# Four LayerNorm tiles on ScalarE, one softmax sum on VectorE, and a new instruction order in a fused attention and token-mixing block

## The chip, the core and the metric

The kernel runs on one core of one Trainium2 chip. The metric is device time in microseconds (us) of one execution. Six executions of the kernel before the change took 207.69 to 209.28 us, with a median of 208.07 us.

## The reference

All inputs are bfloat16. There is one batch, S = 2048 positions and D = 512 features.

```python
mod = (silu(c) @ w_mod).reshape(1, 6, 1, 512)        # sa, ca, ga, sb, cb, gb
h = layernorm(x) * (1 + ca) + sa
x = x + ga * A(h)                                     # A: sliding attention
h = layernorm(x) * (1 + cb) + sb
x = x + gb * B(h)                                     # B: MLP over positions

def A(x):   # 32 heads of 16; each position looks at 8 positions: itself and 2, 4 .. 14 before it
    q, k, v = split(x @ wqkv)
    logits = einsum('bhsd,bhswd->bhsw', q, kg) * 16 ** -0.5    # positions before 0 masked
    return einsum('bhsw,bhswd->bhsd', softmax(logits), vg) @ wo

def B(x):
    h = layernorm(x)
    u = gelu(einsum('bsd,sf->bdf', h, w1) + b1)       # F = 1792, the sum runs over positions
    return (einsum('bdf,fs->bds', u, w2) + b2).transpose(0, 2, 1)
```

So there are three norms in a row: the first feeds the attention, the second follows it, and the third is the one inside B. Because B sums over all positions, its first product can begin for early positions while the attention of later positions is still being computed.

## The kernel before

The 2048 positions are 16 tiles of 128. They are worked in five chunks of 2, 4, 4, 4 and 2 tiles (`SIZES`). A chunk of four tiles has 512 columns, one of two tiles has 256. Each step is added to a graph under a name with its engine (`G.add`, lines 50 to 83); in the names the first number is a tile, a chunk, or a chunk and a part. For each chunk:

- `ln1s<tile>` (line 628, by `ln_stats`, line 368) takes mean and variance of a tile of x with `bn_stats` and `bn_aggr` on VectorE. `rstd1_*` (ScalarE) and `nb1_*` (VectorE) make scale and bias of a group, and `n1_<tile>` applies them. Which engine applies the norm of which tile is a letter in `NE` (A is ScalarE, D is VectorE, P is GpSimd).
- The tiles are transposed: in chunks 0 and 1 by TensorE (`tr*`) and copies out of PSUM (`hT*`), in chunks 2 to 4 by a transposing DMA (`xt<tile>`, line 637).
- `qkv<chunk>_<t><j>` are the products for q (t = 0), k (1) and v (2), 16 matmuls of 512 columns for four values of j in chunks 1 to 3; `ev*` copies each out of PSUM, mostly on ScalarE. `wsc<t>_<k>` scales a weight block by 1 + ca before its first use.
- `qk<chunk>_<0..3>` on VectorE multiplies q by the eight shifted copies of k, one multiply of 4096 elements a partition in a chunk of four tiles; `red*` on TensorE sums the products over the head's features. `max*` (VectorE), `sub*` (TensorE) and `exp*` (ScalarE) follow. `esum*` is the sum of the eight exponentials, made by eight matmuls with the identity, lines 766 to 769; `rcp*` (ScalarE) its reciprocal as exp(-ln), and `smB*` (VectorE) the scaling.
- `a2_*` and `vd*` are DMAs that lay out the weights and v, `pv<chunk>_<0..3>` on VectorE multiplies them, `pvacc*` on TensorE sums over the window, `oev*` (ScalarE) copies out, and `wo<tile>` is the output product plus x. `x1_<tile>` takes it out of PSUM with its row sum, `ln2q<tile>` its sum of squares (both on ScalarE, by `accum_out`), then second norm (`n2_*`, `aff*`) and third norm (`ln3s*`, `h3_*`).

B's first product is `mlp1_<part>_<ft>_<first tile>` (line 921): for 14 blocks ft of F it sums over the tiles of `h3`, in parts with parked sums (`park*`, `inj*`, `padd*`), so that it fills TensorE during the attention. `gelu<ft>` follows, then `mlp2_<tile>` over the 14 blocks, `fin<tile>` on VectorE and the store.

The order in which all engines are fed is not derived at build time: it is the text `ORDER` (line 182). `schedule` (lines 85 to 116) reads it name by name, and each engine executes its own instructions in that order. A suffix chooses the engine (`:a`, `:d`, `:p`) or, with `:q`, the form of a matmul step: `mm` (lines 500 to 504) then emits each matmul as four matmuls of 32 weight columns, on the four column strips of the array:

```python
        for j in range(0, P, 32):
            nc.tensor.matmul(out[j:j + 32], lhsT=lhsT[:, j:j + 32], rhs=rhs, tile_position=(0, j), **kw)
```

This document calls that form column-tiled, and the other plain. `red*` and `pvacc*` are column-tiled always (line 738 and line 803). The token `fill:2:114` emits 114 matmuls of 128 columns whose result nobody reads; `warm*` emits nine of these. The durations, latencies and byte counts that stand in the `add` calls are not read by `schedule`: they leave the emitted program as it is.

PSUM has six slots for matmul results (pool `ps`), and `big` has four buffers for the products of `qk*` and `pv*`; the slot of each step also follows from `ORDER`.

Of the kernel before, what the change touches and what calls it, by code (L numbers as in the profile page):

```python
# [7 lines left out]
ACT = mybir.ActivationFunctionType  # L8
# [33 lines left out]
class _Graph:  # L42
# [7 lines left out]
    def add(self, eng, dur, fn, **kw):  # L50
        return self.add_any([(eng, dur, fn)], **kw)
# [131 lines left out]
ld_x_1_2 ident ld_c act_table ld_x_1_4 ld_x0 consts warm2 ld_x_2_8 ld_x1 cps ld_x_2_6 silu_exp ld_wmod1 ln1s3  # L183
ld_wqkv1 ln1s5 ld_wqkv0 ld_x_3_10 ln1s4 ln1s2 ln1s0 rstd1_1 ln1s1 ld_wmod0 ln1s9 rstd1_0 nb1_0 nb1_1 silu_dve
n1_1 n1_0 ld_x_4_14 ln1s6 n1_5 n1_2 fill:2:114 tr0_0 ln1s8 modcols1 n1_3 halo0 ld_wqkv2 n1_4 hT0_3:a hT0_1:d
hT0_0:a ld_x_3_12 fill:4:11 tr1_2 a1col hT0_2:d wsc1_0:a wsc1_1:d tr1_0 ld_wo3 wsc1_3:d wsc1_2:d hT1_3:a ln1s7
qkv0_12 hT1_1:a ld_wmod5 wsc0_0:a wsc0_1:d qkv0_10 wsc0_3:d ld_b2 rstd1_2 wsc0_2:d ln1s10 ld_wmod4 hT1_0:a
qkv0_00 ev0_10:a ln1s11 ev0_12:a modcols0 ld_wo0 nb1_2 qkv0_02 sab hT1_2:d ld_wmod3 n1_6 qvb0 ln1s15 qkv1_02
qvb_cp0 ln1s14 wsc2_2 ev0_02:a qvb1 ln1s13 wsc2_3 qkv1_10 wsc2_1:a wsc2_0:a qvb_cp1 qk0_3 qkv1_00 ev0_00:a
qkv0_22 qk0_2 ev1_02:a qkv1_01 ev1_10:a qk0_0 qkv0_20 ev1_01:a qk0_1 ev1_00:a red0_0 xt6 qkv1_12:q n1_9 qk1_0  # L190
ev0_20:a red0_1 red0_2 ld_wo1 red0_3 mask ev1_12:a ld_wmod2 qkv1_13:q n1_7 qkv1_03 max0 n1_8 xt7 qk1_2 qkv1_11
ev1_03:a xt9 sub0 qkv1_23 ev1_11:a exp0 qkv1_21 qk1_1 ev1_13:a xt8 ev0_22:a esum0 qkv1_22:q ld_b1 rcp0 halo_v1:p
rstd1_4 vd0_1 smB0 qkv1_20 qk1_3 a2_0_1 modcol2 a2_0_0 ev1_20:a red1_0 ev1_23:a a2_0_2 red1_1 ev1_22:a red1_2
a2_0_3 ln1s12 red1_3 ev1_21:a ld_wo2 qkv2_00 mcols0 nb1_4 max1 rstd1_3 n1_14 vd0_0 n1_15 qkv2_10 vd0_2 nb1_3
ev2_00:a n1_10 sub1 pv0_1 ev2_10:a xt10 qkv2_01 n1_12 qk2_0 mrowt0 qkv2_02 exp1 vd1_3 qkv2_11 vd0_3 ev2_01:a
n1_11 vd1_2 qkv2_22 pv0_2 ev2_11:a xt12 qkv2_12 mrows0:a ev2_02:a qk2_1 pvacc0_2 xt11 ev2_12:a red2_0 n1_13
esum1:q halo_v2:p xt13 qkv2_13:q rcp1 qk2_2 ev2_22:a qkv2_03:q vd1_1 ev2_13:a qkv2_23:q ev2_03:a smB1 qkv2_20:q
qk2_3 a2_1_3 red2_1 ev2_20:a a2_1_2 qkv3_01:q halo_k3:a ev2_23:a a2_1_0 red2_2 a2_1_1 qkv3_13 pv0_0 ld_w1_0_896
red2_3 st_row0 pv0_3 ev3_13:a qkv2_21:q vd1_0 max2 pvacc0_0 ev2_21:a qkv3_10:q pv1_3 pvacc0_1 sub2:q oev0_0:a
qkv3_23:q ev3_10:a exp2 qkv3_00:q ld_row0 pv1_2 xt14 ev3_01:a qkv3_02:q ev3_00:a qkv3_20:q vd2_0 ev3_23:a vd2_1  # L200
esum2:q pv1_0 ld_w1_0_0 qkv3_21 rcp2 pvacc0_3 qkv3_03:q woq_s oev0_2:a ev3_02:a pvacc1_3 ev3_03:a smB2 qkv3_11:q
pv1_1 a2_2_2 wo1:q ev3_11:a a2_2_1 ev3_21:a wo0 xt15 x1_1 halo_v3:a qk3_1 pvacc1_1 oev1_3:a a2_2_0 pvacc1_0 x1_0
a2_2_3 qkv3_12 oev1_1:a ld_w1_0_512 oev1_0:a qk3_0 pvacc1_2 vd2_2 modcol3 oev1_2:a vd2_3 ev3_12:a ln2q0 wo4
qk3_3 wo5 x1_4 ln2q1 qkv4_12 mcols1 ev3_20:a qk3_2 red3_0 ln2q4 red3_1 qkv3_22:q ln2m0 wo3 ev3_22:a pv2_1 x1_5
mrowt1 wo2:q mrows1:a x1_3 st_row1 red3_2 pv2_0 x1_2 pvacc2_1 rstd2_0 red3_3 ln2q2 qkv4_02:q oev2_1:a ld_row1
nb2_0 max3 n2_0 vd3_3 ev4_02:a vd3_0 pv2_3 sub3 vd3_2 qkv4_10 exp3 pvacc2_0 n2_1 esum3 pv2_2 ln2q3 qkv4_20
ev4_12:a qkv4_22:q rcp3 ev4_20:a ln2m2 pvacc2_2 aff0 warm3 oev2_0:a oev2_2:a qkv4_00:q smB3 rstd2_2 ln2q5 nb2_2
pvacc2_3 ln3s0 a2_3_1 n2_2 warm1 ev4_22:a a2_3_0 ln3s1 n2_3 biascols oev2_3:a a2_3_2 ln2m4 ev4_10:a aff2 wo7:q
a2_3_3 rstd2_4 ld_w2_1 rstd3_0 wo6:q nb2_4 nb3_0 ln3s2 n2_4 n2_5 h3_0 vd3_1 ln3s3 wo8:q h3_1 x1_6 aff4 warm0
rstd3_2 x1_7 wo9:q nb3_2 ln3s4 h3_2 h3_3 x1_8 ln3s5 halo_v4:p mlp1_0_2_0:q vd4_1 ev4_00:a pv3_0 mlp1_0_5_0:q  # L210
x1_9 mlp1_0_1_0:q rstd3_4 ln2q9 mlp1_0_0_0:q nb3_4 pv3_3 biascols_cp:a vd4_2 h3_5 pvacc3_0 h3_4 mlp1_0_6_0:q
ln2q8 mlp1_0_0_4:q pv3_2 mlp1_0_1_4:q vd4_3 park0_0:a mlp1_0_5_4:q mlp1_0_2_4:q park0_1:a mlp1_0_4_0:q ln2q7
park0_2:a pv3_1 mlp1_0_3_0:q vd4_0 ln2q6 mlp1_0_3_4:q oev3_0:a pvacc3_2 park0_3:a ld_w1_0_1152 pvacc3_3 oev3_2:a
ln2m6 mlp1_0_4_4:q qk4_0 oev3_3:a pvacc3_1 rstd2_6 mlp1_0_7_0:q oev3_1:a nb2_6 qk4_2 red4_0 n2_9 mlp1_0_6_4:q
wo13:q n2_7 qk4_1 ld_w1_0_1408 n2_6 wo12:q qk4_3 n2_8 park0_4:a red4_1 red4_2 aff6 red4_3 ld_w2_3 park0_5:a
wo11:q x1_12 mlp1_0_9_0:q ln2q12 park0_6:a wo10:q max4 x1_11 ld_w2_0 ln3s8 x1_13 sub4:q mlp1_0_10_0 ln3s7 exp4
x1_10 ln3s6 esum4 mlp1_0_11_0 ln3s9 rcp4 mlp1_0_12_0 smB4 rstd3_6 ln2m12 a2_4_3 ln2q10 h3_7 mlp1_0_8_0 h3_6
a2_4_1 rstd2_12 h3_8 mlp1_0_8_4 ln2q13 a2_4_2 nb2_12 h3_9 n2_12 ln2q11 a2_4_0 ln2m13 mlp1_0_9_4 ln2m10 rstd2_13
aff12 mlp1_0_7_4 rstd2_10 nb2_10 ln2m11 mlp1_0_7_8 ln3s12 rstd2_11 mlp1_0_8_8 n2_10 mlp1_0_9_8 pv4_0
ld_w1_0_1664 mlp1_0_11_4 park0_7:a rstd3_12 nb2_13 pv4_2 mlp1_0_10_4 park0_8:a n2_13 mlp1_0_10_8 nb2_11 pv4_1  # L220
mlp1_0_11_8 park0_9:a ld_w1_1_0 mlp1_0_12_4 park0_10:a pv4_3 mlp1_0_12_8 park0_11:a pvacc4_2 pvacc4_0 park0_12:a
aff10 pvacc4_1 pvacc4_3 n2_11 mlp1_0_13_0 aff13 ld_w2_5 oev4_0:a mlp1_0_13_4 aff11 oev4_2:a mlp1_0_13_8 inj1_0
wo15 ln3s10 wo14 ln3s13 rstd3_10 ln3s11 park0_13:a mlp1_1_0_6 x1_15 ld_w1_1_640 rstd3_13 ld_w1_1_896 rstd3_11
ln2s15 inj1_4 inj1_2 inj1_3 mlp1_1_3_6 nb3_13 h3_10 rstd2_15 nb2_15 mlp1_1_2_6 x1_14 n2_15 ln2s14 h3_13
mlp1_1_3_10 inj1_1 mlp1_1_0_10 mlp1_1_1_6 aff15 rstd2_14 nb2_14 mlp1_1_2_10 ln3s15 n2_14 mlp1_1_4_6 park1_0:a
h3_12 mlp1_1_1_10 aff14 inj1_5 rstd3_15 inj1_6 mlp1_1_4_10 mlp1_1_5_6 ln3s14 ld_w1_1_1408 mlp1_1_6_6 h3_11
rstd3_14 h3_15 park1_1:a h3_14 mlp1_1_6_10 mlp1_1_5_10 park1_2:a mlp1_1_10_10 ld_w1_2_0 park1_3:a mlp1_1_9_10
park1_4:a padd1_10 park1_5:a mlp1_1_7_10 park1_6:d ld_w2_7 mlp1_1_12_10 mlp1_1_8_10 padd1_12 padd1_9 mlp1_2_1_11
padd1_7 ld_w1_2_640 mlp1_2_1_14 gelu9 mlp1_2_2_11 gelu7 mlp1_2_4_11 ld_w2_4 gelu10 mlp1_2_4_14 mlp1_2_0_11
gelu12 padd2_4 mlp1_2_2_14 padd2_1 mlp1_2_0_14 padd2_2 mlp1_2_3_11 ld_w2_9 padd2_0 mlp1_2_3_14 gelu1 mlp1_2_6_11  # L230
padd1_8 gelu0 mlp1_2_5_11 padd2_6 gelu4 gelu2 mlp1_2_5_14 padd2_3 mlp1_1_13_10 padd2_5 gelu6 ld_w2_2 gelu8
mlp1_1_11_10 padd1_13 gelu5 gelu3 mlp2_0_0 padd1_11 gelu11 ld_w2_11 mlp2_0_0b gelu13 mlp2_0_0c mlp2_4_0 fin0_0
st_out0_0 mlp2_2_0 mlp2_8_0 fin2_0 fin4_0 st_out2_0 mlp2_1_0 st_out4_0 ld_w2_13 fin8_0 mlp2_7_0 fin1_0 st_out1_0
mlp2_5_0 st_out8_0 mlp2_11_0 mlp2_3_0 mlp2_6_0 fin3_0 fin5_0 st_out3_0 mlp2_9_0 st_out5_0 fin6_0 fin7_0
st_out6_0 ld_w2_15 mlp2_10_0 fin9_0 st_out9_0 st_out7_0 mlp2_14_0 fin10_0 st_out10_0 fin11_0 mlp2_12_0
st_out11_0 fin14_0 mlp2_13_0 st_out14_0 fin12_0 mlp2_15_0 fin13_0 mlp2_15_1 st_out13_0 fin15_0 st_out12_0
mlp2_15_2 fin15_1 st_out15_0 fin15_2 st_out15_1 st_out15_2
# [4 lines left out]
def kernel(  # L242
# [22 lines left out]
    NE=('PAPADADAAADAAAPA', 'AAPPAPAAAAAAPAAA', 'APPAAADDDDDDDADD'),  # L265
    X1D=(14, 15),
    LN2D=(14, 15),
# [100 lines left out]
    def ln_stats(l, st, src, reads, name):  # L368
        st6, mv = ln_t["st6", l], ln_t["mv", l]

        def fd():
            nc.vector.bn_stats(st6[:, st, :], src)
            nc.vector.bn_aggr(mv[:, st, :], st6[:, st, :])
        return add("dve", 0.86, fd, reads=reads, writes=[("mv", l, st)], name=name)
# [230 lines left out]
    def build_chunk(ch):  # L605
# [26 lines left out]
        if ch in XDMA:  # L632
            first = None
            for sl, st in enumerate(tiles):
                dma_t = lambda sl=sl, st=st: nc.sync.dma_start_transpose(out=hT[:, :, sl * P:(sl + 1) * P],
                                                                         in_=h3[:, st, :])
                add("sp", 1.25, dma_t, reads=[("n1", st)] + ([("hT_raw", bh)] if sl else []),
                    writes=[("hTr", ch, sl)] + ([] if sl else [("hT_raw", bh)]), bytes_=0.5, lat=1.2, desc=8,
                    name=f"xt{st}")
# [378 lines left out]
```

## Time and profile before

| | before |
|---|---|
| median of 6 executions | 208.07 us |
| the profiled execution: device time | 207.69 us |
| its span, first to last instruction | 205.8 us (1.9 us lie around it) |
| TensorE matmul busy | 196.1 us (95%), 2072 instructions recorded |
| VectorE busy | 162.8 us (79%), 258 instructions |
| ScalarE busy | 118.3 us (57%), 271 instructions |
| GpSimd busy | 15.0 us (7%), 36 instructions |
| mean granted TensorE clock | 0.998 |

The page of the profile gives one execution. PE is TensorE's matmul row, PEld its weight loads, DVE is VectorE, ACT is ScalarE, POOL is GpSimd and SP the queue that issues nearly all DMAs. A matmul's end is modelled and overlaps the next one, so a busy PE says only that matmuls follow each other; how fast they do is seen from their starts. All steps are emitted through one helper, so every row has the same source line, L133, and rows are told apart by the buffers they write and read (`big<-q_sb,k_f` is `qk*`, `big<-a2sb,vD` is `pv*`, `st<-xx` are the statistics). Engines execute their own queue in order, so the names of `ORDER` can be laid on the recorded instructions one by one; times of named steps in this document come from that.

### The profile page before, as it was taken

To read this page: it belongs to the slowest core of one execution; us is meant where nothing else is said; L and a number is where in the kernel's file an instruction comes from. 1 tells how busy PE (TensorE), PEld (TensorE's weight loads), DVE (VectorE), ACT (ScalarE), POOL (GpSimd) and SP (SyncE) were. 2 spreads that over 40 slices of the span, in tenths; PEclk is the share of its full clock that TensorE was granted. 3 is DMA by queue.
4 is the path that set the end of the run, shared out by engine and by line. 5 is a ranking of instruction groups with operands and counts; after the bars stand their busy time and mean duration, and the time that the engine had idled before them with its cause. 6 is when DMAs were issued, how large, how long until landed. Compare 5 with 4: busy or idle time off the path is not lost.

```text
span 205.8 us, 5065 instructions
## 1 busy us (share of the span) xinstructions
PE 196.1 (95%) x2072; PEld 107.4 (52%) x2089; DVE 162.8 (79%) x258; ACT 118.3 (57%) x271; POOL 15.0 (7%) x36
## 2 busy tenths in 40 slices
PE   7999999997999997999999999999999999999994
PEld 6998645453553645644555444444444444444453
DVE  2989999999999999999999999974574262067845
ACT  2396897982778778989999796673682000000000
POOL 4112007010000000231000100000000000000000
PEclk9999999999999999999999999999999999999999
DMA  5999584796769919073479249649993045006202
GB/s 169 306 373 308 140 169 118 194 293 171 236 212 272 304 64 353 29 170 143 148 187 238 38 78 329 214 120 271 268 299 96 29 116 165 0 25 161 84 25 78
DMA packets 55114, 35.98 MB, mean 175 GB/s; under 512 B 24628, under 2 KB 52404, under 8 KB 55092
## 3 DMA queue, kind: packets, MB, share of 16 engines
q1 hardware_dynamic: 55084, 35.67, 61.3%
q8 instruction: 16, 0.26, 0.6%
q14 instruction: 6, 0.05, 0.1%
q10 hardware_dynamic: 8, 0.00, 0.0%
HBM read 22.55 MB, written 2.10 MB: 120 GB/s over the span
## 4 chain that ended last, share of the span: by engine, by line
PE 39%; DVE 33%; ACT 10%; issue 6%; DMA 5%; SPq 4%; DVEq 0%; ACTq 0%
PE psS L133 38%; DVE big L133 15%; DVE h L133 7%; DVE st L133 6%; SPq L133 4%; DVE mv L133 2%; ACT h L133 2%; DMA vD<-v_sb 2%; DMA a2sb<-lsb 1%; DMA xx<-in_A_x_dram 1%; ACT xx L133 1%; ACT v_sb L133 1%; PE psL L133 1%; ACT k_f L133 1%; ACT junk L133 1%
## 5 line engine op out<-in xcount | busy, mean ns | idle before, releaser
L133 PE MATMUL psS<-h,wst 128*32 128x512 bf16 (+1 forms) x369 | 50.7, 379 | 0.7 <-POOL h L133 0.2
L133 PE MATMUL psS<-hT,w_qkv 128*32 128x512 bf16 (+3 forms) x511 | 46.7, 345 | 1.8 <-DMA hT<-h 1.4
L133 PEld LDWEIGHTS <-wst 128*128 128x128 bf16 (+1 forms) x476 | 29.7, 98 | 30.2 <-issue 2.2
L133 PEld LDWEIGHTS <-w_qkv 128*32 128x32 bf16 (+1 forms) x558 | 29.8, 109 | 22.2 <-issue 4.2
L133 DVE TENSOR_TENSOR big<-a2sb,vD 128x4096 bf16<-128x4096 bf16 (+1 forms) x20 | 36.5, 1860 | 0.6 <-DMA vD<-v_sb 0.2
L133 DVE TENSOR_TENSOR big<-q_sb,k_f 128x4096 bf16<-128x4096 bf16 (+1 forms) x20 | 36.4, 1860 | 0.0
L133 DVE SCALAR_TENSOR_TENSOR h<-psS,bcol,rows_bc 128x512 f32<-128x512 f32 (+2 forms) x18 | 12.4, 690 | 23.2 <-PE psS L133 22.9
L133 PE MATMUL psS<-gT,big 128*128 128x512 bf16 x111 | 24.8, 379 | 0.1
L133 PEld LDWEIGHTS <-ident 128*128 128x128 bf16 (+1 forms) x301 | 16.0, 106 | 6.7 <-issue 2.1
L133 PEld LDWEIGHTS <-big 128*128 128x128 bf16 x144 | 12.0, 97 | 13.2
L133 ACT ACTIVATE h<-xx,nb,rs 128x512 bf16<-128x512 bf16 x22 | 17.2, 809 | 1.9 <-DVE nb L133 1.9
L133 PE MATMUL psS<-woq,o_sb 128*32 128x512 bf16 (+1 forms) x181 | 16.2, 380 | 0.6 <-ACT xx L133 0.4
L133 DVE TENSOR_TENSOR psS<-psS,gT 128x512 f32<-128x512 f32 x14 | 9.0, 694 | 8.0 <-PE psS L133 8.0
L133 DVE BATCH_NORM_STATS2 st<-xx 128x6 f32<-128x512 bf16 x18 | 12.2, 676 | 3.7 <-DMA xx<-in_A_x_dram 3.6
L133 PE MATMUL psS<-ident 128*128 128x128 bf16 x161 | 12.5, 248 | 1.4 <-POOL epscol L133 1.4
L133 ACT ACTIVATE v_sb<-psS,qvb 128x512 bf16<-128x512 f32 (+1 forms) x20 | 11.2, 599 | 4.6 <-PE psS L133 4.2
L133 ACT ACTIVATE lv<-mv,epscol 128x1 f32<-128x1 f32 (+2 forms) x25 | 7.3, 292 | 10.9 <-DVE mv L133 10.8
L133 ACT ACTIVATE q_sb<-psS,qvb 128x512 bf16<-128x512 f32 (+1 forms) x20 | 11.1, 600 | 2.8 <-DVE qvb L133 1.9
L133 DVE TENSOR_TENSOR h<-h,xx 128x512 bf16<-128x512 f32 (+2 forms) x18 | 11.4, 633 | 1.6 <-DMA out_dram<-h 1.0
L133 ACT ACTIVATE gT<-psS,bcol 128x512 bf16<-128x512 f32 x14 | 8.7, 685 | 7.0 <-DVE psS L133 7.0
L133 PEld LDWEIGHTS <-group 128*32 128x32 bf16 x288 | 7.1, 96 | 9.0 <-DVE big L133 2.6
L133 DVE TENSOR_TENSOR h<-h,rows_bc 128x512 bf16<-128x512 bf16 (+2 forms) x20 | 11.4, 580 | 0.3
(89 smaller groups left out, 213.4 us busy)
## 6 DMA issues: line engine op xcount, KB each, us to landing
vD<-v_sb SPq DMA_DIRECT2D x12, 524.5 KB, 4.8
big<-in_B_w_dram SPq DMA_DIRECT2D x4, 896.0 KB, 8.2
vD<-v_sb SPq DMA_DIRECT2D x8, 268.5 KB, 2.8
wst<-in_B_w_dram SPq DMA_DIRECT2D x3, 640.0 KB, 4.4
out_dram<-h SPq DMA_DIRECT2D x15, 128.0 KB, 1.8
xx<-in_A_x_dram SPq DMA_DIRECT2D x7, 256.0 KB, 6.4
wst<-in_B_w_dram SPq DMA_DIRECT2D x2, 800.0 KB, 4.8
gT<-in_w_mod_dram SPq DMA_DIRECT2D x3, 512.0 KB, 8.4
```

The costliest lines, as they stand in the source:

```text
L133: r = fn(*a, **k)
```

## The change

Five things differ. `LN1A` lists tiles 10 to 13: their first-norm statistics are two ScalarE activations with accumulated sums (mean, and mean of squares), and a small VectorE step `ln1v<tile>` that makes the variance from the two. `ESD` lists chunk 4: its `esum4` is a VectorE reduction over SBUF instead of eight matmuls into PSUM. `NE` gives other engines to some norms. Two planning numbers (a latency and a byte count) change, which the emitted program does not contain. And `ORDER` is another text: other suffixes and another order on every engine.

```diff
-    NE=('PAPADADAAADAAAPA', 'AAPPAPAAAAAAPAAA', 'APPAAADDDDDDDADD'),
+    NE=('PAPAAPAADAAPAAPD', 'PAPAAPAAAADAAADP', 'APPAAADDDDADAADA'),
     X1D=(14, 15),
+    ESD=(4,),
+    LN1A=(10, 11, 12, 13),
...
     def ln_stats(l, st, src, reads, name):
         st6, mv = ln_t["st6", l], ln_t["mv", l]
+        if l == 0 and st in LN1A:
+            def fa():
+                nc.scalar.activation(junk[:], src, ACT.Identity, scale=1.0 / D, accum_out=mv[:, st, 0:1])
+                nc.scalar.activation(junk[:], src, ACT.Square, scale=D ** -0.5, accum_out=st6[:, st, 0:1])
+            add("act", 1.36, fa, reads=reads + ["act_table"], writes=[("sq", l, st)], name=name)
+            add("dve", 0.15, lambda: nc.vector.scalar_tensor_tensor(
+                mv[:, st, 1:2], mv[:, st, 0:1], mv[:, st, 0:1], st6[:, st, 0:1], op0=ALU.mult, op1=ALU.subtract,
+                reverse1=True), reads=[("sq", l, st)], writes=[("mv", l, st)], name="ln1v" + name[4:])
+            return
...
-        add("pe", 8 * max(0.06, _t_mm(SB)), f, reads=[("lsb", b), "ident"], alloc=s_s, name=f"esum{ch}")
+        if ch in ESD:
+            add("dve", 0.15 + 0.00104 * NW * SB, lambda: nc.vector.tensor_reduce(
+                ls, _ap(ee[:, 0, 0:1], [[1, SB], [SB, NW]]), mybir.AxisListType.X, ALU.add),
+                reads=[("lsb", b)], writes=["ls"], name=f"esum{ch}")
+        else:
+            add("pe", 8 * max(0.06, _t_mm(SB)), f, reads=[("lsb", b), "ident"], alloc=s_s, name=f"esum{ch}")
```

The two orders begin as follows (before, then after):

```diff
-ld_x_1_2 ident ld_c act_table ld_x_1_4 ld_x0 consts warm2 ld_x_2_8 ld_x1 cps ld_x_2_6 silu_exp ld_wmod1 ln1s3
-ld_wqkv1 ln1s5 ld_wqkv0 ld_x_3_10 ln1s4 ln1s2 ln1s0 rstd1_1 ln1s1 ld_wmod0 ln1s9 rstd1_0 nb1_0 nb1_1 silu_dve
-n1_1 n1_0 ld_x_4_14 ln1s6 n1_5 n1_2 fill:2:114 tr0_0 ln1s8 modcols1 n1_3 halo0 ld_wqkv2 n1_4 hT0_3:a hT0_1:d
...
+consts ld_x_1_2 act_table ld_x0 ld_x_1_4 ld_c ld_x_2_8 ld_x1 ident ld_x_2_6 ld_wmod1 ln1s3 halo0 ld_wqkv1 cps
+ln1s2 warm2 ld_wqkv0 silu_exp ld_wmod0 ln1s0 ln1s4 ln1s1 ln1s5 rstd1_0 ld_x_4_14 nb1_0 ln1s9 rstd1_1 n1_0 n1_1
+silu_dve nb1_1 ld_wqkv2 ln1s8 fill:2:70 tr0_0 n1_2 n1_4 modcols1 ln1s7 hT0_3:a n1_5 n1_3 ld_x_3_10 hT0_2:d a1col
...
```

The column-tiled steps fall from 50 to 19, and none is left among the `qkv*`, `sub*` and `esum*` of chunks 0 and 1 (four were there: `qkv1_12`, `qkv1_13`, `qkv1_22` and `esum1`). The changes of form between neighbouring steps on TensorE are 34 before and 35 after. Fillers fall from 114 + 11 to 70 + 16 matmuls. Copies and weight scalings that go from ScalarE to VectorE are `ev0_12`, `ev0_02`, `wsc0_0`, `wsc2_0` and `wsc2_1`; `hT0_1` goes the other way. `halo_v1`, `halo_v2` and `halo_v4` go from GpSimd to ScalarE, `halo_k3` the other way. The transposing DMAs of chunk 3 stand on the SP queue ahead of the second chunk's `a2_1_*`, as before, but behind other neighbours: before they follow `vd1_3`, `vd0_3` and `vd1_2`, after they follow `ld_wo3`, `ld_wo2`, `ld_wo0` and `vd0_3`.

## The prediction

> **What bounds the kernel now.** I read the slices first, then TensorE's own waits, then the stretches, then the timeline around the longest waits. Slices of the page, and two stretches:
>
> ```profile
> PE   7999999997999997999999999999999999999994
> DVE  2989999999999999999999999974574262067845
> ```
> ```profile
> 13.50:137.50 124.00, 119.12 (x1574) 64.61 (x1586) 120.69 (x179) 100.13 (x241) 11.18 (x12) 1.00 0.69 192
> 137.50:200.00 62.50, 62.13 (x287) 28.46 (x291) 29.86 (x45) 11.97 (x20) 0.00 (x0) 1.00 0.48 130
> ```
>
> The busy columns are PE, PEld, DVE, ACT, POOL. From 13.5 to 137.5 us two engines are full at once, TensorE (119.1 of 124.0) and VectorE (120.7); after 137.5 only TensorE (62.1 of 62.5). TensorE has real work from 13.46 (`qkv0_12`) to about 202. Starts of successive plain 512-column matmuls lie 216 ns apart, a column-tiled set of four takes 0.215 (16 in 0.86, between 89.18 and 90.04), and each of the 34 changes of form costs 0.095 (311 ns instead of 216). Summed, the work is 178.9 us and the changes 3.2; the rest, some 6 us, is waiting. The waits are few (in us: total, times, longest):
>
> ```profile
> PE psL L133 <- DVE m L133: 1.5, 1, 1.5
> PE psS L133 <- DMA hT<-h: 1.4, 1, 1.4
> PE psS L133 <- ACT xx L133: 0.4, 1, 0.4
> PE psS L133 <- POOL h L133: 0.2, 1, 0.2
> ```
> ```profile
> 2.62 8.57 PE L133 MATMUL psS<-ident 128*128 128x128 bf16 x114
> 11.02 0.61 PE L133 MATMUL psS<-ident,h 128*128 128x128 bf16 x8
> 13.46 1.24 PE L133 MATMUL psS<-hT,w_qkv 128*128 128x256 bf16 x7
> ...
> 46.88 0.60 PE L133 MATMUL psL<-big,group 128*32 128x512 bf16 x8
> 48.88 1.06 PE L133 MATMUL psS<-hT,w_qkv 128*32 128x512 bf16 x16 [1.40 <-DMA hT<-h]
> ...
> 76.74 1.05 PE L133 MATMUL psS<-hT,w_qkv 128*32 128x256 bf16 x32
> 79.27 0.59 PE L133 MATMUL psL<-m,nident 128*128 128x512 bf16 x2 [1.49 <-DVE m L133]
> ```
>
> The wait at 47.1 is `qkv3_01` for a transposing DMA; the one at 77.5 is `sub3` for `max3`, which VectorE ends at 79.22 because it comes late from its `pv` products. The smaller ones (0.2 to 0.5 between starts, near 75, 91, 93, 97, 108, 124 and 137) are also for something that stands late on VectorE. So TensorE's sum is the floor, and VectorE's position sets how far above it the end lies: at `pvacc4_3` (124.2) TensorE waits for VectorE's last `pv4_3`, and from there only 77.5 us of TensorE work and the stores remain.
>
> **The change part by part.** Rows used:
>
> ```profile
> L133 DVE BATCH_NORM_STATS2 st<-xx 128x6 f32<-128x512 bf16 x18 | 12.2, 676 | 3.7 <-DMA xx<-in_A_x_dram 3.6
> L133 ACT ACTIVATE junk<-xx 128x512 bf16<-128x512 bf16 x14 | 8.7, 623 | 0.1
> L133 DVE TENSOR_REDUCE m<-psL 128x64 bf16<-128x512 f32 x2 | 1.4, 684 | 0.0
> L133 DVE SCALAR_TENSOR_TENSOR mv<-sums 128x1 f32<-128x1 f32 x4 | 0.6, 153 | 0.0
> L133 PEld LDWEIGHTS <-wst 128*128 128x128 bf16 x276 | 23.8, 99 | 24.6 <-issue 1.2
> L133 PEld LDWEIGHTS <-wst 128*32 128x32 bf16 x200 | 5.9, 97 | 5.6 <-issue 1.0
> ```
>
> Neighbours on one engine overlap by some 0.08, so in a full queue a tile's statistics take 0.80 (8.50 to 9.29), the tiny step 0.10 with its dependency, an ACT pass with a sum 0.61, a CAST out of PSUM 0.60, a weight scaling on VectorE 0.26.
>
> *Form of the matmuls.* 31 steps go back to plain: 0.216 against 0.215 for the same columns, nothing. Changes of form 34 to 35: +0.1. `esum4` leaves TensorE: eight matmuls of 64 columns at 29 ns, -0.2. The page "TensorEngine Tiling (Array Packing)" of the Trainium skill (Restrictions and Gotchas) says that column tiling is mutually exclusive with fast weight load. By it plain weight loads should be cheaper; the rows have 99 ns for a load of 128 columns and 97 for each of four loads of 32, and both lie under the matmuls, so that this rule is worth 0 in the trace.
>
> *Start.* VectorE's statistics begin at 3.58 for both. Chunk 0's tiles stand third and fifth instead of fifth and sixth, and `nb1_0` ahead of `ln1s9`. By steps of 0.80 `n1_0` ends near 9.4 (before 10.30) and `n1_1`, behind `rstd1_1` on ScalarE, near 9.85 (10.27). The fillers decide next: `ident` now stands behind `consts` on GpSimd, whose instructions take 1.7 us, so TensorE begins at 3.15 instead of 1.44, but `warm2` and the fill are 79 matmuls instead of 123. In the trace matmuls of 128 columns start 107 ns apart until 6.90, then 56. If the granted clock rises at 6.90 again, the fill ends at 9.5; if it rises 5.5 us after the first matmul, as here, 8.65, then near 10.4. The page "TensorE: Matmul & The Clock Gate" (Part 1) speaks against the later start: it wants one full free-running window of about 3.4 us, which puts the rise anywhere from 3.4 to 6.8 us after the start. An estimate by that page has the fill end between 9.4 and 11.0. I take 10.3 from the rows. Behind that, ScalarE does `hT0_3`, `n1_3`, `hT0_0`, `hT0_1` and `wsc1_0` in line, 10.95 to 13.33, so the first useful matmul comes at 13.4, against 13.46 with 0.3 of waits in it: -0.35. Bounds: -0.45 (then `n1_4` holds ScalarE) and +2.0 (all 79 fillers at 107 ns). `ld_c` behind the 1.28 us table load is hidden if the sequencer issues it during the load; if not, TensorE begins near 3.8 and 0.65 comes on top.
>
> *VectorE up to its first attention product* (`qk0_*`, before at 20.33). Gone: statistics of tiles 10, 11 and 13, 3 x 0.80 = 2.4, one norm 0.33, `hT0_1` 0.2. New: `ev0_12`, `ev0_02` 1.2, three `wsc` 0.8. Net -0.95; its waits there are 0.85 before. To find them after, I laid the new order of each queue out with the step times above and compared, step by step, when an operand is made with when its user is reached: 0.75 (0.25 of it for `modcols0`). It begins `qk0_0` near 19.25: -1.1.
>
> *VectorE from there to `pv4_3`.* Gone: `ln1s12` 0.8. New: four `ln1v` 0.4, `esum4` 0.6 (nearest row the reduction of the same 512 elements from PSUM, 0.60 in a queue; low end 0.35, the 128x512 bf16 scaling), `n2_10` 0.33. Net +0.5. Its waits in this stretch are 1.9 before; the same walk gives 0.35 at `nb1_3`, which waits for ScalarE's `rstd1_3` with `max1` and `pv0_0` queued behind it, and small ones later; I take 1.6 (bounds 0 and 4.0). `esum4` itself waits for `exp4` (109.2, a microsecond early), and its `rcp4` has the 1.6 of `ln3s7` and `ln3s6` to finish under before `smB4`. So `pv4_3` ends 1.1 - 0.5 + 0.3 = 0.9 earlier, near 123.2.
>
> *What TensorE's waits become.* Before, chunk 3's four transposes shared SP's queue with three `vd` DMAs, and the last, `xt13`, was issued at 45.29 and used 3.6 later. Now one `vd` stands among them, their norms are ready by 39.5, all are issued by 42.0 and landed by some 44.5, and `qkv3_00` comes at 46.4: those 1.5 go. They are not kept: by the walk `mrowt1` then waits some 0.3 for `mcols1`, `sub3` still waits 0.6 for `max3`, `esum3` 0.5 for `exp3`, `pvacc2_0` 0.5 for `pv2_0`, the first `mlp1` 1.0 for `h3_2` and `h3_3`, `pvacc3_3` 0.8 for `pv3_3`, `pvacc4_3` 0.45. Each is TensorE arriving earlier at the same VectorE. `vd1_2` waits on SP until `ev1_23` (44.1) with `a2_1_*` behind it, which are due only after `smB1` (45.5): hidden.
>
> *ScalarE* gets 4 x 2 x 0.61 = 4.9 for the statistics and loses 3.4 of copies and scalings; norms and halos move both ways. Its copies for `qk1_1` and `rcp0` come 0.3 and 0.05 before VectorE needs them, so cover ends there at once (rival 2).
>
> *After `pv4_3`* TensorE's remaining work is 77.3 instead of 77.5 (one more step stands ahead): -0.2; the wait for the last third-norm tile at 137.2 goes, since `h3_14` comes near 135 and `mlp1_1_9_10` needs it only at 136: -0.25. Parks, `padd`, `gelu` and stores lie beside TensorE as before.
>
> Sum: -0.9 - 0.2 - 0.25 = -1.35 against the profiled execution's own 207.69 (span 205.8 and 1.9 around it), that is 206.3. That execution was the fastest of six, 0.38 below their median, so on the median I predict 206.7.
>
> **Rivals.** (1) *TensorE's waits really go*: VectorE loses only 0.8 to waits and ScalarE is never late; another 0.8 comes off at `pv4_3`, 0.1 at the start and 0.3 of small waits from 137 to 150: 205.5. For it: few waits are above 0.15 in the trace of before. Against: VectorE was full too. (2) *ScalarE becomes late*: between 20 and 32 it is busy 10.88 of 12.0. The statistics add 4.9 there and just behind, 2.85 leave (two `wsc`, `ev0_02`, one norm) and 1.1 is free: up to 0.95 late at `rstd1_3` and at the `ev2_*` copies that `qk2_0` needs, so that VectorE's lead of 1.1 is gone. 0.3 to 0.4 is left: 207.7. (3) *Slower, by the clock of the fill*: TensorE starts late and its fillers stay at 107 ns. Each slow filler costs 0.051; with all 79 slow, and `c_t` held back by the table load, `tr0_0` starts at 13.2 instead of my 10.3, ScalarE's line of copies behind it slides with it (its 0.3 of slack aside), and all later work shifts by 2.6: 209.3. The gain is lost from a fill that ends after 11.7. Against it: here the clock rose 5.5 us after the first matmul, and the fill would need 8.8 at the slow rate. (4) *The named parts do nothing*, because they lie beside the bound and only the order counts. That is true of the form (0.1), not of the statistics, which stood in VectorE's full queue; were it so, what is left is the transposes' wait given back in smaller ones: 208.0.
>
> **How the numbers follow.** My case has 0.50, rival 1 0.12, rivals 2 and 4 together 0.24, rival 3 0.14. A measurement here can tell about 0.5% (1.04 us) from no change, so faster means below 207.03. My case's own range is 206.0 to 207.5, and some five sixths of it lie below that: 0.42, with rival 1: 0.54. Same: the rest of my case and most of rivals 2 and 4: 0.29. Slower: rival 3 and a few cases of a ScalarE later than rival 2 has it: 0.17. The range goes from 205.0, a little below rival 1, to 209.2, which cuts rival 3 near its end and leaves less than 2 in 10 outside.
>
> **What would show it.** Right: first useful matmul near 13.4; `qk0_0` near 19.3; no wait of TensorE for the transposing DMA; VectorE's last `pv` ending near 123; the wait for `m` below 1. Wrong: matmuls 107 ns apart up to the first transpose, VectorE idle for k and q copies between 23 and 33, or a wait for a DMA that I call hidden.

## The result, and the profile after

| | before | after |
|---|---|---|
| median, runs side by side | 207.94 us (48 executions, 206.98 to 209.78) | 207.08 us (22 executions, 206.18 to 207.78) |
| the profiled execution: device time | 207.69 us | 207.27 us |
| its span | 205.8 us | 205.3 us |
| TensorE matmul busy, instructions recorded | 196.1 us, 2072 | 193.0 us, 1635 |
| VectorE busy | 162.8 us | 163.2 us |
| ScalarE busy | 118.3 us | 120.5 us |

The ratio after to before is 0.9953, with a 95% interval of 0.9939 to 0.9968: the change gains 0.86 us between the medians, where 1.35 was forecast. The interval leaves out no gain at all, so the gain is small but real; it is under the 0.5% (1.04 us) that the prediction had counted as no change. A second measurement of the same kernel (below) gives 0.9952.

The slices of the page after, TensorE and VectorE:

```profile
PE   3999999989999997989899999999999999999994
DVE  2999999799999999999999999975574204369365
```

The two stretches as in the prediction, from the first useful matmul (busy columns PE, PEld, DVE, ACT, POOL):

```profile
13.24:137.50 124.26, 118.93 (x1178) 62.81 (x1193) 120.61 (x181) 102.90 (x253) 8.40 (x11) 1.00 0.70 194
137.50:200.00 62.50, 62.18 (x289) 28.77 (x294) 30.73 (x45) 11.36 (x18) 0.00 (x0) 1.00 0.45 130
```

The picture is the same: TensorE and VectorE both full until 137, TensorE alone after that. What moved is where the waits stand. TensorE's waits after (total, times, longest):

```profile
PE psS L133 <- POOL epscol L133: 3.1, 1, 3.1
PE psL L133 <- DVE big L133: 1.1, 1, 1.1
PE psS L133 <- DVE big L133: 1.0, 2, 0.7
PE psL L133 <- DVE m L133: 0.7, 1, 0.7
PE psS L133 <- POOL h L133: 0.7, 1, 0.7
PE psS L133 <- ACT lsb L133: 0.6, 1, 0.6
PE psS L133 <- ACT gT L133: 0.5, 1, 0.5
```

The first line is the later begin of the fill. The wait for the transposing DMA (1.4) is gone and the one for `m` has halved. In their place stand waits for VectorE's products (`big`), for a third norm (`h`), for `exp3` (`lsb`) and for a parked sum (`gT`). TensorE's timeline after, at the places shown of before, and at the new waits:

```profile
3.19 6.38 PE L133 MATMUL psS<-ident 128*128 128x128 bf16 x79
9.65 0.91 PE L133 MATMUL psS<-ident,h 128*128 128x128 bf16 x8
...
13.24 1.39 PE L133 MATMUL psS<-hT,w_qkv 128*128 128x256 bf16 x11 [0.26 <-ACT w_qkv L133]
...
46.37 1.05 PE L133 MATMUL psL<-big,group 128*32 128x512 bf16 x16 [1.05 <-DVE big L133]
...
47.57 1.70 PE L133 MATMUL psS<-hT,w_qkv 128*128 128x512 bf16 x6
...
80.44 0.59 PE L133 MATMUL psL<-m,nident 128*128 128x512 bf16 x2 [0.74 <-DVE m L133]
...
102.36 0.61 PE L133 MATMUL psS<-big,group 128*32 128x512 bf16 x8 [0.74 <-DVE big L133]
```

Chunk 3's first product, `qkv3_00`, now runs at 47.57 without a wait; but at 46.37 TensorE has already waited 1.05 for VectorE. VectorE's timeline says where that came from:

```profile
35.05 1.22 DVE L133 TENSOR_REDUCE m<-psL 128x128 bf16<-128x1024 f32 x1
37.35 2.36 DVE L133 TENSOR_TENSOR big<-a2sb,vD 128x2048 bf16<-128x2048 bf16 x2 [1.09 <-DMA a2sb<-lsb]
```

Before, the same stretch read:

```profile
35.54 1.22 DVE L133 TENSOR_REDUCE m<-psL 128x128 bf16<-128x1024 f32 x1
37.37 1.23 DVE L133 TENSOR_TENSOR big<-a2sb,vD 128x2048 bf16<-128x2048 bf16 x1
```

VectorE, at 35.05 still 0.5 ahead of before (`max1` began at 35.54), stands idle from 36.27 to 37.35: `pv0_0` waits for the copied probabilities of chunk 0. The chain of the page (in order of time: start, length, what) shows the last of the four copies, `a2_0_1`, issued on SP at 33.62 and awaited for 3.61 us:

```profile
33.62 3.61 DMA a2sb<-lsb
```

Before, `pv0_1` needed the same copies, the last of them issued at 35.35. Its landing, 2.0 later at 37.35, came just in time for the start at 37.37. So most of the lead was lost in one DMA wait that stood in no row of before.

### The profile page after: what moved, and what is told of

The parts are those of the page before. It is cut to its first block, busy times and chain, and to the rows that moved or that the text cites. A ratio compares the mean times of both kernels' runs of the same rounds, so it can differ in the third digit from the quotient of the medians.

```text
span 205.3 us, 4203 instructions
## 1 busy us (share of the span) xinstructions
PE 193.0 (94%) x1635; PEld 102.6 (50%) x1655; DVE 163.2 (79%) x260; ACT 120.5 (59%) x283; POOL 13.0 (6%) x36
## 4 chain that ended last, share of the span: by engine, by line
PE 53%; DVE 28%; issue 6%; DMA 6%; SPq 3%; ACT 2%; DVEq 0%
PE psS L133 52%; DVE big L133 16%; DVE st L133 4%; DVE h L133 3%; SPq L133 3%; DMA wst<-in_B_w_dram 2%; DMA a2sb<-lsb 2%; DMA xx<-in_A_x_dram 1%; DVE mv L133 1%; ACT h L133 1%; PE psL L133 1%; DVE m L133 1%; DVE lsb L133 1%; DVE ls L133 0%; DVE nb L133 0%
## 5 line engine op out<-in xcount | busy, mean ns | idle before, releaser
L133 PE MATMUL psS<-h,wst 128*128 128x512 bf16 (+1 forms) x249 | 50.3, 379 | 1.4 <-POOL h L133 0.7
L133 PE MATMUL psS<-hT,w_qkv 128*128 128x512 bf16 (+3 forms) x305 | 45.9, 339 | 0.6 <-ACT w_qkv L133 0.3
L133 PEld LDWEIGHTS <-wst 128*128 128x128 bf16 (+1 forms) x356 | 28.7, 98 | 32.2 <-issue 3.2
L133 PEld LDWEIGHTS <-w_qkv 128*128 128x128 bf16 (+1 forms) x354 | 29.5, 111 | 21.2 <-issue 3.1
L133 PEld LDWEIGHTS <-ident 128*128 128x128 bf16 (+1 forms) x203 | 12.9, 107 | 6.0 <-issue 2.9
L133 ACT ACTIVATE h<-xx,nb,rs 128x512 bf16<-128x512 bf16 x19 | 15.1, 808 | 0.8 <-DVE nb L133 0.7
L133 ACT ACTIVATE junk<-xx 128x512 bf16<-128x512 bf16 x22 | 13.8, 627 | 0.2
L133 POOL TENSOR_SCALAR h<-xx,rs,nb 128x512 bf16<-128x512 bf16 x9 | 7.3, 813 | 100.4 <-DVE nb L133 83.6
L133 DVE BATCH_NORM_STATS2 st<-xx 128x6 f32<-128x512 bf16 x14 | 9.5, 676 | 3.8 <-DMA xx<-in_A_x_dram 3.8
L133 ACT ACTIVATE k_f<-psS 128x512 bf16<-128x512 f32 x15 | 8.9, 594 | 5.6 <-PE psS L133 5.6
```

The lines of the kernel that those rows point to most:

```text
L133: r = fn(*a, **k)
```

## Experiments: the parts of the change

**Statistics back on VectorE.** In the kernel after:

```diff
-    LN1A=(10, 11, 12, 13),
+    LN1A=(),
```

> The changed kernel with the statistics of tiles 10 to 13 back on VectorE, at the same places of the order; the rest of the change stays. Theory (VectorE's queue up to pv3_3 sets the end, and the four statistics stood in it): four times 0.80 come back and four small steps of 0.13 go, so pv3_3 moves from 102.3 to about 105 and the time rises by 1.8 to 2.7 us over the changed kernel's 207.1, to 208.9 to 209.8. Rival (only the order counts, ScalarE is as full as VectorE): within 0.3 us of 207.1.

Measured: 210.22 us, ratio to before 1.0117 (1.0086 to 1.0149); against the kernel after by the two ratios 1.65%, some 3.4 us slower, in the profiles 2.8. VectorE's first scores begin at 21.35 instead of 19.41. Of these 1.9, 1.1 is a wait of TensorE for the modulation's weights, which the profile after does not have, and 0.8 the statistics of one tile. From there to `pv4_3` VectorE has 2.15 us more work, but here it does not wait for the copied probabilities, for which it waits 1.1 in the kernel after. So the two waits of 1.1 offset each other, and the 2.8 fit the 0.8 and 2.15 of the four statistics by that luck. The direction is shown; with four executions and two waits that differ, the exact price is not.

**The statistics alone, in the order of before.** `LN1A` and the small steps are added to the kernel before, and nothing else is moved:

> The kernel before with only the statistics part of the change: the sums of tiles 10 to 13 by ScalarE (two passes each), one small VectorE step each instead of two large ones, in the written order of before. Theory (VectorE sets the pace from the first scores to the last product): about 0.7 us less on VectorE per tile, 0.13 back, so VectorE's work falls by 2.2 us, and the time by 1 to 2.2 us, to 205.4 to 206.6. Rival (ScalarE's 1.4 us per tile delays the evictions that VectorE and TensorE wait for): the gain is 0 or a loss of up to 1.5 us, with new waits for ScalarE's evictions or normalisation steps in the stretch from 20 to 48 us.

Measured: 209.63 us, ratio 1.0092 (1.0062 to 1.0122): the rival holds. VectorE lost 2.0 us of work (160.8 busy instead of 162.8), but ScalarE does `ln1s10` and `ln1s11` at 15.17 and 17.50, ahead of `ev0_12`, which slips from 16.27 to 18.88. TensorE waits 0.8 for a copy of k, and VectorE's idle time between its first scores and `pv4_3` rises from 1.6 to 2.9. (The profile is of the slowest of the six executions, whose clock falls for a while from 19.8 on, as the last section shows; the late copy and TensorE's wait lie ahead of that, the idle time behind it.) With the run before: taking the statistics off VectorE pays only in an order that places them where ScalarE has room, and that order is slower without it.

**The short fill, taken out and put in.** `fill:2:70` becomes `fill:2:114` in the kernel after, and the other way in the kernel before:

> The kernel after, with the first stretch of fill matmuls put back from 2x70 to 2x114. Theory (the shorter fill lets the first transpose, and with it all that follows, start earlier): 88 matmuls by about 56 ns put 2.5 us on the end of the fill, from 9.4 to about 11.9; the first transpose waits for the fill instead of the first normalised tile (9.65) and starts at about 11.9; the start moves later by up to 2.2 us, and what is left at the end is 1.5 to 2.2 us: 208.6 to 209.3. Rival (the front of the kernel is set by VectorE, which normalises the first tiles anyhow, and the fill's end has slack): at most 0.4 us, 207.1 to 207.5, with the first reduction of scores still near 19.4.

> The kernel before, with its first stretch of fill matmuls cut from 2x114 to 2x70 and nothing else. Theory (the fill's end at 11.0 set the first transpose): the transpose goes at the first normalised tile, about 10.3, and the first reduction of scores comes earlier by 0.3 to 0.7 us: 207.2 to 207.6 against a kernel before of 207.4 to 207.9. Rival (the first useful matmul waits for the weights of the modulation, not for the fill): no change, within 0.2 us. Third: the clock rises later with less fill, and 1 us or more is lost.

Measured: 208.19 us in the first, ratio 1.0022 (0.9998 to 1.0046), so 0.7% or 1.4 us slower than after; 208.56 us in the second, ratio 1.0006 (0.9973 to 1.0039), no gain. TensorE's timeline, first the kernel after with the long fill, then the kernel before with the short one:

```profile
3.19 9.74 PE L133 MATMUL psS<-ident 128*128 128x128 bf16 x123
12.77 0.61 PE L133 MATMUL psS<-ident,h 128*128 128x128 bf16 x8
...
15.71 1.50 PE L133 MATMUL psS<-hT,w_qkv 128*128 128x256 bf16 x12
```
```profile
10.43 0.62 PE L133 MATMUL psS<-ident,h 128*128 128x128 bf16 x8 [2.06 <-POOL h L133]
...
13.42 1.57 PE L133 MATMUL psS<-hT,w_qkv 128*128 128x256 bf16 x10 [0.45 <-ACT w_qkv L133]
```

After, the long fill holds the first transposes to 12.77 and the first product to 15.71 (13.24). Before, the short fill leaves TensorE idle for 2.06, and the first product still starts at 13.42 (13.46), since ScalarE scales the weights only then, and the first scores at 20.29 (20.33). (Its profile also has a wait of 1.1 for the copies of chunk 0, so the order of before can meet one too; the median speaks for the fill only within its wide interval.) In the new order TensorE begins 1.75 later, so the shorter fill is what keeps that from showing; by itself it is worth nothing.

**No `:q` at all.** Every `:q` is stripped from the kernel before; only `red*` and `pvacc*` stay column-tiled:

> The kernel before with every column-tiled set of four small matmuls issued as the plain kind; the order is the same, and the number of changes between the two kinds of matmul goes from 34 to 49. Theory (a change costs TensorE 0.095 us and TensorE's stream shows in the time): up to 15 x 0.095 = 1.4 us slower, less where TensorE waits anyhow, so 0.3 to 1.4 us. Rival (form costs nothing on the path before the middle of the kernel, because VectorE sets the pace there): within 0.2 us. If the plain form itself were slower or faster, the groups' mean durations (216 and 215 ns) would differ.

Measured: 207.13 us, ratio 0.9968 (0.9946 to 0.999): not slower, so the price of 1.4 us does not show at the end. It is not shown to be nothing on TensorE either. In this profile `qkv3_01` does not wait for the transposing DMA and starts at 48.06 (before 48.88); `pvacc3_1`, the last sum of chunk 3, starts at 103.35 (103.25). In between TensorE needs 0.9 us more than before, about ten changes' worth, which the missing wait pays for. Why that DMA was in time here stays open.

**`esum4` back on TensorE**, in the kernel after:

```diff
-    ESD=(4,),
+    ESD=(),
```

> The changed kernel with esum4 made by eight matmuls again. Theory: after pv3_3 TensorE runs without a break but for one wait of 0.5 at 113, for park0_6, which stands on ScalarE behind rcp4, which waits 0.8 for VectorE's esum4. That wait goes and 0.23 of matmuls comes back: 0.25 less, 206.8 us, and VectorE's pv4_3 comes 0.9 earlier with no effect on the end. Rival A (VectorE still sets the end at pv4): 0.9 less, 206.2. Rival B (the sum on VectorE pays): 0.2 to 0.3 more, 207.3.

Measured: 207.25 us, ratio 0.9967 (0.9945 to 0.9989); from the start of `pvacc3_3` to that of the last `fin` step 100.02 against 99.96. The step is worth nothing either way. Its wait is only exchanged: after, `rcp4` waits 0.8 for the VectorE sum, `park0_6` stands behind it on ScalarE and TensorE waits 0.48 for the slot; here TensorE waits 0.31 for ScalarE's `ls` right behind the eight matmuls instead.

**The parked sum ahead of `rcp4`**, in the kernel after: `park0_6` is moved before `rcp4` in `ORDER`.

> The changed kernel with one ScalarE copy, park0_6, ahead of rcp4 and not behind it; esum4 stays on VectorE. Theory (TensorE's wait of 0.5 at 113 is for the PSUM slot that this copy frees): the wait goes and the end comes 0.4 to 0.5 us earlier, 206.6. Rival (TensorE would only wait later, for VectorE's pv4 or h3): 207.0 to 207.1.

Measured: 206.42 us, ratio 0.9971 (0.9951 to 0.9991). The wait of 0.48 goes and one of 0.25 for a third norm comes at 114.51; from `pvacc3_3` to the last `fin` step it is 99.97, as after. Its median is lower, but its profile has no wait for the copied probabilities, which this edit does not touch; so the next runs go to that wait. Why 8 of its 12 executions lie below 206.8 stays open.

## Experiments: the wait for the copied probabilities

**Later loads of the output weights.** `ld_wo3` and `ld_wo2`, which follow the copies on SP, are moved behind `xt11`:

> The changed kernel with the two loads of the output weight, ld_wo3 and ld_wo2, issued behind xt11 and no longer right behind the four a2_0 DMAs. Theory (they share the DMA engines with a2_0, whose last piece lands 3.6 us after its issue, and VectorE waits 1.1 us for it at pv0_0): the landing falls to about 2.0 to 2.5 us, the wait to 0.2 or less, and the kernel gains 0.7 to 1.0 us: 206.1 to 206.4. Rival (the landing is slow for what is ahead of it, the transposes and vd0_2): the wait stays near 1.1 and the time near 207.1.

Measured: 207.05 us, ratio 0.9981 (0.9962 to 1.0); the profile has no wait at `pv0_0`, but the times still run from 206.25 to 207.87. That speaks against those loads as the cause, though the copies here were also issued 0.4 us later than in the kernel after.

The packet records of the traces show another one. About once in 250 weight loads and matmuls (3290 recorded, 13 packets) a 16 KB packet of the kind "instruction" passes on queue q8; in the kernel after such a packet takes 0.9 to 1.3 us. One of them begins at 35.0 to 35.7 us in all eight profiles compared from here on. The copies are 1024 packets of 128 bytes, so each of the 16 DMA engines has 16 of each of the four, if they are spread evenly. In the records:

| run | instruction packet | 128-byte packets behind it | idle before `pv0_0` |
|---|---|---|---|
| after | 35.05 to 36.18 | 16 | 1.09 |
| after with `esum4` on TensorE | 35.11 to 36.17 | 16 | 1.15 |
| after with later loads | 35.69 to 36.61 | 0 | none |
| after with the parked sum first | 35.19 to 36.15 | 0 | none |

Where the wait is, 16 packets, one engine's share of one copy, leave in the 0.3 us after the instruction packet's end. The landing events, 16 for each copy, say the same: for the last copy 15 lie at 35.38 to 35.63 in the kernel after and one at 37.23; with the parked sum first all 16 lie at 35.27 to 35.53. That the packet and the 16 pieces were on one engine is inferred from this, since the records do not name a packet's engine. Nor is it the whole delay: from the last piece to the last landing event 0.8 to 1.0 us pass in the profiles with the wait and 0.3 in those without, for which no run gives a reason. Three runs put this to the test, the first of them the kernel after, unchanged.

> The kernel after, unchanged, as the measure for the two below. Its times so far spread from 206.2 to 207.8, and two profiles of its kind show either a wait of 1.1 us for the first product of probabilities and values (a 16 KB instruction packet holds one DMA engine from 35.05 to 36.18 and the last pieces of the copied probabilities leave behind it) or none. Theory (the spread is that packet): times in two groups about 1 us apart, near 206.4 and 207.4. Rival (the spread has nothing to do with it): no groups.

Measured: 207.31 us (206.19 to 207.82), ratio 0.9952 (0.993 to 0.9975). Three of 12 executions lie below 206.6, eight from 207.24 to 207.82, one between. The 22 executions of the first measurement show no such gap (no step between neighbours is above 0.21), so two groups are suggested and not shown. Its profile has the wait, 16 packets behind an instruction packet of 35.04 to 36.44, and VectorE's line:

```profile
37.62 2.36 DVE L133 TENSOR_TENSOR big<-a2sb,vD 128x2048 bf16<-128x2048 bf16 x2 [1.40 <-DMA a2sb<-lsb]
```

**Fewer, wider fill matmuls**, to move the instruction packet:

```diff
     def fill_fn(k, n):
-        for _ in range(n):
+        nw = 18 if n == 70 else 0
+        for _ in range(nw):
+            nc.tensor.matmul(psS[k][:, 0:2 * P].rearrange("p (a b) -> p a b", a=2), lhsT=ident[:],
+                             rhs=ident.unsqueeze(1).to_broadcast([P, 2, P]), start=True, stop=True)
+        for _ in range(n - 2 * nw):
```

> The kernel after, with 36 of the 70 fill matmuls of the first stretch replaced by 18 of twice the width: the same TensorE time (2 x 56 ns against about 110), 18 matmuls fewer. The instruction packets of TensorE come after fixed numbers of its instructions, so the one at 35.05 us should come 18 matmuls later in the program, at about 37 to 38 us, when the copied probabilities have landed. Theory (this packet makes the wait of 1.1 us): the first product starts within 0.1 us of the end of the row maximum in every run, the upper group of times vanishes, and the median falls by 0.6 to 0.9 us against the kernel after, to 206.2 to 206.5. Rival (the wait has another cause, or another packet takes its place): median and spread as those of the kernel after, within 0.2 us.

Measured: 207.58 us (206.2 to 208.72), ratio 0.9967 (0.994 to 0.9995). The premise failed: the packet came at 35.36, in the same place, with 16 packets behind it and a wait of 1.5. Its place does not simply follow the count of matmuls issued, and this run does not tell the theories apart.

> The run with 18 wide fill matmuls, and every column-tiled set of four small matmuls issued as the plain kind: 35 to 37 changes of form, about 150 matmuls and two instruction packets fewer. Theory (form and changes of form cost nothing that shows, few packets mean few collisions): within 0.3 us of the run with wide fill alone, either side. Rival (a change costs 0.095 us and the plain sets are no shorter): 0.2 us slower; or the column-tiled sets in the second half gain something, and it is 0.5 us or more slower.

Measured: 206.58 us (206.42 to 207.86), ratio 0.9933 (0.9906 to 0.9959). Its median is not slower, but that is set by how few executions have the wait: six of the eight lie at 206.4 to 206.7, where the lowest three of the run with wide fill alone are 206.2 to 206.7, so that a cost of 0.2 us for form and changes is not excluded. Two lie above 207.4, and the profiled one (207.86) has the wait, 1.39, behind a packet of 35.27 to 36.48. Why fewer of its executions meet the packet stays open.

**One copy on another queue.** What cannot be moved can be forestalled: in the kernel after, one of the four copies is issued by ScalarE, early.

```diff
+            act_q = (ch, jj) == (0, 1)
-            add("sp", 0.6, lambda jj=jj: nc.sync.dma_start(
+            add("act" if act_q else "sp", 0.6, lambda jj=jj, q=nc.scalar if act_q else nc.sync: q.dma_start(
```

In `ORDER`, `a2_0_1` moves to just behind `smB0`.

> The kernel after, with one of the four copies of chunk 0's probabilities issued from ScalarE's queue, right behind its last statistics pass (about 31.95 us), instead of last on SyncE's queue (33.62). SyncE's third and last copy is then issued at 32.96. The copies' packets should have left by about 34.7, before the 16 KB instruction packet that came at 35.0 to 35.4 in every profile of the kernel after. Theory (that packet, holding one DMA engine for about 1.1 us, makes the first product wait): the product starts within 0.1 us of the end of the row maximum, the times near 207.3 vanish, and the median falls to 206.3 to 206.6, 0.7 to 0.9 below the kernel after (207.1 to 207.3). ScalarE pays 0.6 us for the issue, of which about 0.5 fits in its wait for the statistics of the last tile. Rival 1 (the wait has another cause): median and spread as in the kernel after. Rival 2 (the issue on ScalarE delays the last normalisation factors and with them the row maximum): the maximum ends 0.5 us or more later and the gain is half or less.

Measured: 206.46 us (206.16 to 207.03, 12 executions), ratio 0.9938 (0.9912 to 0.9965), as the theory had it. ScalarE issues the copy at 31.61, the last 128-byte packet goes at 34.62, and the instruction packet, at 34.98 to 36.38, finds none to hold up. VectorE's timeline, with no idle time before the product:

```profile
35.01 1.22 DVE L133 TENSOR_REDUCE m<-psL 128x128 bf16<-128x1024 f32 x1
36.14 2.71 DVE L133 TENSOR_TENSOR big<-a2sb,vD 128x2048 bf16<-128x2048 bf16 x2
```

The row maximum is not later, so rival 2 falls. None of the 12 executions is above 207.03, where the kernel after has 8 of 12 above 207.2 in its second measurement, and the two runs with low medians that leave the copies as they are have 4 of 12 and 2 of 8. The missing upper part, not the median, is what speaks for the edit. What is left of TensorE's waits for VectorE's products has no 1.1 in it:

```profile
PE psS L133 <- DVE big L133: 1.0, 2, 0.7
PE psL L133 <- DVE m L133: 0.7, 1, 0.7
```

The medians put it 0.6 to 0.85 us below the kernel after. The ratios to the kernel before (0.9938 here, 0.9952 there) point the same way, but differ by 0.3 us only and their intervals overlap, since the kernel before was 0.5 faster beside this run (207.66). The run shows that an earlier copy ends the wait. It would do so whatever held up the last pieces: that it is the instruction packet rests on the records, five profiles with 16 pieces behind it and the wait, three with none and no wait.

## Why the prediction was right, and where it was not

The forecast of 206.7 (205.0 to 209.2) lies 0.4 below the median measured, and the gain was two thirds of that forecast; at -0.47% it falls just inside the 0.5% that the text had counted as no change, so the likeliest of the three chances, a gain beyond that, did not come.

- *Form of the matmuls: nothing, changes of form +0.1.* Not contradicted: without `:q` the kernel before gets no slower at its end, though TensorE needed 0.9 more on the way. A price of 0.1 was below what the runs can tell.
- *Start, -1.1.* Held: the first useful matmul came at 13.24 (predicted 13.4), `qk0_0` at 19.41 (19.25, before 20.33). `ld_c` was issued during the table load. The fill ended at 9.4 and not at 10.3, because the clock rose 3.9 us after the first matmul; the first normalised tile then set the transposes. Rival 3's place was real, its price smaller: with the fill ending at 12.8 the kernel loses 1.4.
- *VectorE from there to `pv4_3`.* The work term held (+0.5 predicted, 102.27 to 102.74 measured), and the sum of the waits came out by luck: 1.6 taken, 1.58 measured. Before has 1.56 counted the same way and not 1.9, so the 0.3 that the prediction gained here was never there. The place was wrong too. The step-by-step walk had 0.35 at `nb1_3`, where the profile after has 0.09; 1.1 of the 1.58 is the wait for `a2_0_1`, which the prediction does not name, and without it 0.5 is left. This is the step that failed: "the same walk gives 0.35 at `nb1_3` ... and small ones later". `pv4_3` ended at 123.73, 0.43 earlier than before, not 0.9.
- *What TensorE's waits become.* The wait of the transposes went, as said. Predicted and measured: `sub3` 0.6 and 0.7, `esum3` 0.5 and 0.6, `pvacc2_0` 0.5 and 0.2, first `mlp1` 1.0 and 0.7, `pvacc3_3` 0.8 and 0.7; `mrowt1` (0.3) and `pvacc4_3` (0.45) did not wait. One more was missed: `red2_1` with 1.05 up to 46.37, the echo of the wait at `pv0_0`, which is gone in the run with the copy on ScalarE's queue. The prediction laid all small waits of before to VectorE; its own rows give 0.4 of them to ScalarE and 0.2 to GpSimd.
- *`esum4` hidden behind a microsecond of slack.* Wrong: it took 0.9 in its queue, not 0.6, and `rcp4` waited 0.8 for it, TensorE 0.48. It cost nothing all the same, since the wait is only exchanged for another.
- *After `pv4_3`, -0.45.* Measured -0.34 from the start of `pvacc4_3`, but the end is set earlier: from the start of `pvacc3_3` to the end of the last `fin` step it is 100.6 to 100.9 us in every run in the new order that is shown here, whatever happened before, and 101.0 to 101.2 in the old. In the new order the product `pv3_3` that `pvacc3_3` waits for, and not `pv4_3`, is therefore VectorE's last word. (In the old order `pvacc3_3` is not that step: `pv3_3` had ended 3.8 us before it, and the last sum of chunk 3 is `pvacc3_1`.)
- *Sum, -1.35 against the profiled execution.* That execution came to -0.42 (its span to -0.55). Without the wait at `pv0_0`, as in the run with the copy on ScalarE's queue, the span is 204.4 against 205.8: -1.4. That is the number of the sum but not its terms: there VectorE waits 0.5 and not 1.6, and `pv4_3` ends 1.29 earlier and not 0.9. So the DMA wait is what stands between the kernel after and the forecast, and the allowance of 1.6 had room for it only by luck. The median lies between, since only a part of the executions meets the wait; how large a part is not shown.

Rival 1 (205.5) fell because TensorE's waits were replaced as listed; even the run without the DMA wait stays at 206.46. Rival 2 fell because VectorE never waited for ScalarE's late steps: its idle time between `qk0_0` and `pv4_3` is the one DMA wait and gaps of at most 0.15. Rival 4 fell with the run that puts the statistics back.

## What to carry to other kernels

A part of a change has no price of its own when the order was made for it: the statistics on ScalarE gain in the new order and lose in the old, the short fill is needed in one and useless in the other. When an operand that comes by DMA is used soon after it lands (here 2.6 us after the issue of a copy that lands in 2.0 when nothing holds it up), its slack is part of the critical path, and its price can be a spread of the times that one profile cannot show; issuing one piece earlier on a second queue took the upper part of that spread away. Look for the one step (here `pvacc3_3`) from which the rest of the kernel takes the same time in every run of the new order, and price the change up to there.

## What the runs showed of the hardware

*Instruction packets delay data.* The page lists them as a queue of their own; this is the window from 34.9 to 36.8 us in the kernel after (packets, MB, share of 16 engines' time):

```profile
q1 hardware_dynamic: 410, 0.16, 33.4%
q8 instruction: 1, 0.02, 3.7%
```

3.7% of 16 engines over 1.9 us is 1.1 us of one engine. The page "Runtime: NRT & Kernel Launch" of the Trainium skill (Instruction fetch mechanics) says that instructions stream in blocks of 16 KiB and that crossing a block's end is mostly hidden. It is, for the engine that fetches: TensorE's waits above are all for other engines. But in the five profiles in which copies stand behind such a packet VectorE waits 1.1 to 1.5 us for them, and in the three in which none do it does not wait. Fewer matmul instructions mean fewer of these packets: 16 before, 13 after, 11 without column-tiled `qkv`, `mlp1` and other product steps.

*The clock's rise is not tied to the first matmul.* In 14 profiles the granted clock rises, and the fill matmuls of 128 columns go from 107 to 56 ns apart, between 5.1 and 9.0 us, 2.8 to 5.9 us after the first matmul, in the kernel after alone 3.9 in one profile and 2.8 in another. The page "TensorE: Matmul & The Clock Gate" of the Trainium skill (Part 1) has a free-running window. Its spread agrees better than the 5.5 us carried over from one row, but three of the 14 rises come earlier than the 3.4 us that the prediction took from it (2.8, 2.8 and 3.3).

*The clock can fall back.* In one execution of the run with the statistics alone, after TensorE's wait of 0.8, the granted clock (the column after POOL's) halves for some 3.4 us:

```profile
18.00:19.00 1.00, 0.70 (x18) 0.65 (x17) 0.68 (x4) 0.97 (x5) 0.00 (x0) 1.00 1.09 328
19.00:20.00 1.00, 0.49 (x2) 0.23 (x2) 0.75 (x2) 1.00 (x3) 0.78 (x2) 0.90 1.12 346
20.00:21.00 1.00, 1.00 (x5) 0.38 (x4) 0.00 (x0) 0.97 (x4) 0.58 (x1) 0.50 1.16 253
...
23.00:24.00 1.00, 1.00 (x5) 0.47 (x4) 1.00 (x1) 1.00 (x4) 0.00 (x0) 0.90 0.19 67
```

The other five executions of that kernel kept the full clock and were as slow within 1.2 us, so this is not its reason. Waits of 1.1 to 2.1 in other profiles had no such effect; what sets it off was not tried.
